# Layer 1's activation h·cos h with one pass fewer: turns, a saturating add, no Abs

## The chip, the cores and the metric
The kernel runs on one core of a Trainium2 chip. The time is device microseconds of that core; before it is the median of three runs. Engines are named as in the profile: PE is TensorE's matmul, PEld its weight load, DVE is VectorE, ACT is ScalarE, POOL is GpSimd, SP is SyncE, which issues the transfers.

## What is computed
```python
# q, k, v: 4 batches, 8 heads, 576 positions, 64 dims; w_in 512x2048, w_out 2048x512 per layer
scores = (1 / 8) * q @ k.T
ret = (scores * Dmat) @ v            # Dmat[i, j] = gamma_h ** (i - j) for i >= j, else 0
x = ret as 2304 x 512
h = x @ w1_in;  x = (h * np.cos(h)) @ w1_out                            # layer 1
h = x @ w2_in;  out = (np.maximum(h, 0) + np.log1p(np.exp(-abs(h)))) @ w2_out   # layer 2, a softplus
```

## The kernel before
Every product is made as three products of rounded parts (a high part and a low part, `h` and `l` in the names), so each value that enters a product is first split: ACT copies the high part, DVE or POOL subtracts to get the low one (`sub`, the row of line 317 in DVE's and POOL's lists).

The program has four stretches. First the attention, in 16 tiles of heads that go alone (0 to about 50 us) and 16 more woven in between what follows. Then the first four of sixteen column blocks of layer 1's hidden width, in five groups of tokens (`slot`: 12 matmuls into a PSUM bank called ha, hb, s or o, the activation, then 12 matmuls `acc<-gh,wh`), to about 200 us. Then the other twelve blocks of layer 1 as phase 0 of a scheme that makes 7 products in place of 8 (`quad`: seven groups of six matmuls, `ha<-x,pair`, `hb`, `s`, with additions on DVE and copies `cv` on ACT between them; `unit`: the output products `acc<-gh,pair`), to about 455 us. Then layer 2 in phases 1 and 2, to the end. `x_load` brings x for a phase and makes its sums (`tt`, 768 columns wide, POOL or DVE) and their splits (`x<-tt`).

The activation of layer 1 (`activate`) takes five passes for a bank. `a1` (line 792, ACT): ek = the nearest integer to h/2π. `a2` (796, DVE): er = h − 2π·ek. `a4` (800 on ACT or 803 on DVE): er = |er|. `a5` (806, ACT): sin(π/2 − er), which is cos h. `a6` (809, DVE): the product with h, into the bank (or g, gs). Then `parts` splits the product (835 on ACT, 317 on DVE) for the output matmuls. A DVE, ACT or POOL instruction runs when those before it on its engine are done, so the order of each engine's list decides who waits.

That order comes from a planner (`Plan`): each operation has an engine, a cost, a key (the time by which it is wanted) and its dependencies, and the planner lays out the whole program, the earliest possible start first and the lower key where two are equal. Operations marked POOL_DVE or ACT_DVE go to the engine that the planner's weights (`FLEX`, `FLEX_AD`) favour. The keys hang on the constants at the head of the file; a changed cost or constant can move instructions anywhere in the program.

Of the kernel before, what the change touches and what calls it, by code (L numbers as in the profile page):

```python
# [6 lines left out]

F32 = mybir.dt.float32
F32R = mybir.dt.float32r
I32 = mybir.dt.int32  # L10
U8 = mybir.dt.uint8
AF = mybir.ActivationFunctionType
ALU = mybir.AluOpType
# [14 lines left out]
NS = 9  # L28
HALF_PI = 1.5707963267948966
TWO_PI = 6.283185307179586  # L30
INV_TWO_PI = 0.15915494309189535


def t_mm(n):
# [8 lines left out]
def t_act(n, psum=False):  # L43
    return n / 1400.0 + (0.112 if psum else 0.154)


def t_dve(n):
    return n / 960.0 + 0.068


def t_dve2(n):
    return n / 1920.0 + 0.068
# [8 lines left out]
ACT_DVE = "act or dve"  # L61
# [4 lines left out]
    return layer == 2 or f < FA  # L66


FLEX = 0.801
FLEX_AD = 3.625  # L70
FLEX_2 = 50.0
ROOM = 258.786
SPARE = 1.248
# [6 lines left out]
GB = 2  # L80
PT = 3
R0 = 26.837
WB = (15.287, 22.043)
W3 = (33.576, 10.601, 12.195, 17.928, 32.155)
XW = 15.342
XC = 10.125
LAG_C = 1.399
LAG_S = 0.9
TT = 3
CA = (25.491, 78.45, 5.426, 6.897)  # L90
TURN = 0.6
XS = 51.626
FILL = (2, 5)
EARLY = 17.347
EARLY_2 = 7.642
AHEAD = {}
GAP = 2.0
LO_A = "pool or dve"
END = 3.1
LC = 8.411  # L100
LT = ("o", "s")
OFF = (4.42, 9.944, 21.033, 32.756)
LL = 12.0
LB = 1.9
WARM = 350
DX = 24.051
LEAD = 7.302
W0 = (46.735, 4.788, -1.046)
M0 = 28.072
AK = (4.689, 2.701)  # L110
PAIR_A = 1.48
# [4 lines left out]
SCALE = "pool"  # L116
KK = 1.331
KQ = -0.176
TIE = -8.152
LAG = -3.047  # L120
LEAD_G = 12.021
CX = 0.925
GT = (4, 7)
LS = 9
LEAD_S = 9.902
W4 = (-17.423, -10.623, 13.552, 0.176, 3.559)
W5 = (15.081, 16.579, 8.481, 12.575, 8.762)
PAD = 192
QS = 3

# [1 line left out]
class Plan:  # L132
# [10 lines left out]
    def op(self, eng, dur, key, fn, r=(), w=(), new=(), port=False, nbytes=0):  # L143
        i = len(self.ops)
        deps = set()
        for t in r:
            deps.update(self.writers.get(t, ()))
            self.readers.setdefault(t, []).append(i)
        for t in w:
            deps.update(self.writers.get(t, ()))  # L150
            deps.update(self.readers.get(t, ()))
            self.writers[t] = [i]
            self.readers[t] = []
        for t in (*r, *w):
            self.users.setdefault(t[0], []).append(i)
        for tag, bufs, tile_key in new:
            self.rings.setdefault(tag, (bufs, []))[1].append((i, tile_key))
        deps.discard(i)
        self.ops.append([eng, dur, key, fn, deps, port, nbytes])
        return i  # L160

    def order(self):
# [32 lines left out]
        for _ in range(n):  # L195
            best = None
            for i in can:
                eng, dur, key, _, _, uses_port, _ = self.ops[i]
                if eng == POOL_DVE:
                    f = max(ready[i], port)  # L200
                    t, d, e = min(
                        ((max(f, free[e]), d, e) for e, d in (("pool", t_pool(dur)), ("dve", t_dve(dur)))),
                        key=lambda o: o[0] + (FLEX if ready[i] < ROOM else FLEX_2 if ready[i] < ROOM_3 else FLEX_3) * o[1])
                elif eng == ACT_DVE:
                    t, d, e = min(
                        ((max(ready[i], free[e], port if e == "dve" and uses_port else 0.0), d, e) for e, d in zip(("act", "dve"), dur)),
                        key=lambda o: o[0] + FLEX_AD * o[1] + (SPARE if o[2] == "dve" else 0.0))
                else:
# [57 lines left out]
def retention_moe_moe(ctx, tc, qkv, w1, w2, mask, mtail, dq, dk, out):  # L266
    nc = tc.nc
# [16 lines left out]
    cst = apool("cst", 1)  # L284
# [4 lines left out]
    op = plan.op  # L289
# [11 lines left out]
    hp_t = small.tile([128, 1], F32, name="hp_t")  # L301
# [41 lines left out]
    CM = [M[-1] - TIE]  # L343
    MB = M[-1] + OFF[-1] + LL + 6.0
    for ph in range(3):
# [126 lines left out]
    def weight_out(q, key):  # L472
# [271 lines left out]
    def x_store(m):  # L744
        n, r0, xk = GROUPS[m], R[m], ("x", "a", m)
        for g in range(2):
            dma(lambda g=g: xd[g][:, :, r0:r0 + n], lambda g=g: T[xk][g][:, :, 0:n].bitcast(F32), 512 * n * 4, M[m] + XS + g, r=XT[m], w=[("xd", g, m)])

# [35 lines left out]
    def activate(layer, e, h_k, n, i, K1, dst=None, g_k=None, g_new=(), need=()):  # L784
        kk, rk = ((g, "m", i) for g in ("ek", "er"))
        k_k, r_k = (kk,), (rk,)
        tmp = lambda g, dt=F32: ew.tile([128, n], dt, tag=g, name=g, padded_shape=[128, 512])
        H_ = lambda: e["h"][:, 0:n]
        if layer == 1:
            def a1():  # L790
                e["k"] = tmp("ek", I32)
                nc.scalar.activation(e["k"], H_(), AF.Copy, scale=INV_TWO_PI)

            def a2():
                e["r"] = tmp("er")
                nc.vector.scalar_tensor_tensor(e["r"], e["k"], -TWO_PI, H_(), ALU.mult, ALU.add)  # L796

            def a4(eng):
                if eng is nc.scalar:
                    nc.scalar.activation(e["r"], e["r"], AF.Abs)  # L800
                else:
                    r = e["r"].bitcast(I32)
                    nc.vector.tensor_scalar(r, r, 0x7FFFFFFF, None, ALU.bitwise_and)

            def a5():
                nc.scalar.activation(e["r"], e["r"], AF.Sin, bias=hp_t[:, 0:1], scale=-1.0)  # L806

            def a6():
                nc.vector.tensor_tensor(dst() if dst else H_(), H_(), e["r"], ALU.mult)  # L809

            op("act", t_act(n, True), K1 + 0.1, a1, r=h_k, w=[k_k], new=[("ek", 2, kk)])
            op("dve", t_dve(n), K1 + 0.6, a2, r=h_k + [k_k], w=[r_k], new=[("er", 2, rk)])
            op(ACT_DVE, (t_act(n), t_dve2(n)), K1 + 1.4, a4, r=[r_k], w=[r_k], port=True)
            op("act", t_act(n) + 0.1, K1 + 1.5, a5, r=[r_k, ("cst", "hp")], w=[r_k, ("sin",)])
            op("dve", t_dve(n), K1 + 2.3, a6, r=[r_k, *(h_k if dst else []), *need], w=g_k or h_k, new=g_new)
            K2 = K1 + 2.8
        else:
            for to, z, g_k, g_new, mem in dst if isinstance(dst, list) else [(dst, slice(0, n), g_k, g_new, ())]:
                def a1(to=to, z=z):
                    d = to()  # L820
                    h_ = H_()[:, z]
                    nc.scalar.activation(d, h_ if d.ndim == 2 else h_.rearrange("p (u c) -> p u c", u=2), AF.Softplus)

                o_ = op("act", t_act(z.stop - z.start, True), K1 + 0.1, a1, r=[*h_k, ("ln",)], w=g_k, new=g_new)
                early.extend((o_, m) for m in mem)
            return
        if not dst:
            return parts(e, H_, h_k, n, i, K2, True)

# [106 lines left out]
    def quad(ph, y, s):  # L936
# [43 lines left out]
        product(1, 1, K, True, True)  # L980
        op(ACT_DVE, both, K + DT - EARLY, keep(1, 0, "v"), r=[rk[1], ("qopen",)], w=[(cv, 0)], new=[("cv", 1, cv)])
        product(2, 2, K + DT, True, True)
        product(3, 5, K + 2 * DT, True, True)
        op("dve", t_dve(HN), K + 3 * DT - EARLY_2, lambda: nc.vector.tensor_tensor(R(2), R(2), c["v"][:, 0], ALU.add), r=[(cv, 0)], w=[rk[2]])
        op(ACT_DVE, both, K + 3 * DT - EARLY, keep(3, 0, "5"), r=[rk[3], ("qopen",)], w=[(cv, 0)])
        product(1, 6, K + 3 * DT)
        op(ACT_DVE, both, K + 4 * DT - EARLY, keep(1, 1, "v"), r=[rk[1]], w=[(cv, 1)])
        product(3, 3, K + 4 * DT)
# [233 lines left out]
    def weight_in_s(ph, y, s):  # L1222
# [148 lines left out]
    def moe_a(t, todo):  # L1371
# [168 lines left out]
    for i in range(P0):  # L1540
        k = M[0] + CA[0] + 4 * i * CA[2]
        job(k, convert_ahead, 1, FQ[0] + i, k, CA[2])
    for q in range(NP2):
        k = CM[0] + CA[1] + 4 * q * CA[3]
        job(k, convert_ahead, 2, q, k, CA[3])
    for ph in range(3):
        W = (W3, W4, W5)[ph]
        for y in range(nb):
            k = KI(ph, y, 0) - XC
            job(k, x_load, ph, y, k)  # L1550
            for s in range(NQ[ph]):
                job(KI(ph, y, s), quad, ph, y, s)
                job(KI(ph, y, s) - max(0.1, W[0] if y == 0 and s < 2 else W[1] if y == 0 or ph else XW), weight_in_s, ph, y, s)
                if not ph:
# [5 lines left out]
        for q in range(NQ[ph]):  # L1560
            if ph:
                job(key_s(ph, 0, 0, q) - max(W[4 if q > 1 else 2], 0.1), weight_out_s, ph, q)
            else:
                k = unit_key(0, 0, q) - W3[2]
                job(max(k, (MR if q < 2 else MB) + 0.01), weight_out, FQ[0] + q, k)
# [83 lines left out]
```

## Time and profile before
| | us |
|---|---|
| median of 3 runs | 846.39 (845.26 to 848.43) |
| the profiled execution, its time | 848.93 |
| the profiled execution, its span | 846.8 |
| PE busy in the span | 825.4 (97%) |
| DVE, ACT, POOL busy | 666.9, 550.7, 84.1 |

The time counts about 2.1 us outside of the span of instructions. The profiled execution is 2.5 us slower than the median.

### The profile page before, as it was taken

Reading aid. Unit: us, or ns where it says so; the run is one execution under the profiler, and the core shown is the slowest. Engines: PE = TensorE matmul, PEld = TensorE weight load, DVE = VectorE, ACT = ScalarE, POOL = GpSimd, SP = SyncE. Lnnn points to the kernel's source line nnn. Section 1 sums busy time; section 2 is a strip of 40 time slices with the busy share of each in tenths; the row PEclk is TensorE's granted clock in tenths of the full one; section 3 lists DMA queues with packets and bytes.
Section 4 is the critical chain, followed back from the end, with each engine's and each line's share of the span. In section 5 each row is a group of like instructions: output and inputs, shape, how many; then the busy total and the mean of one; then the engine's idle time right before and its main releaser. Section 6 shows DMA issues by size and latency. Waiting matters only on the chain.

```text
span 846.8 us, 15943 instructions
## 1 busy us (share of the span) xinstructions
PE 825.4 (97%) x5792; PEld 783.1 (92%) x5792; DVE 666.9 (79%) x1486; ACT 550.7 (65%) x1213; POOL 84.1 (10%) x105
## 2 busy tenths in 40 slices
PE   7989999999999999999998999999999999999996
PEld 5767788888999999999998999999999999999996
DVE  3788767978898756876677879779888999876786
ACT  1276655678988867887787767555565766545442
POOL 3522110320231010010101010000000000000000
PEclk9999999999999999999999999999999999999999
DMA  9787999899887878685957866616469584464321
GB/s 313 276 330 253 361 384 331 309 371 352 307 323 224 299 275 267 224 234 203 313 216 242 293 207 206 248 63 232 180 197 352 207 310 153 153 227 168 119 86 53
DMA packets 74654, 208.79 MB, mean 247 GB/s; under 512 B 6864, under 2 KB 30800, under 8 KB 70736
## 3 DMA queue, kind: packets, MB, share of 16 engines
q1 hardware_dynamic: 71120, 203.06, 66.5%
q0 software_dynamic: 3456, 4.72, 3.7%
q8 instruction: 45, 0.74, 0.4%
q14 instruction: 33, 0.27, 0.1%
HBM read 129.64 MB, written 78.12 MB: 245 GB/s over the span
## 4 chain that ended last, share of the span: by engine, by line
PE 68%; issue 17%; DVE 6%; DMA 4%; ACT 3%; POOL 1%; SPq 0%; POOLq 0%; DVEq 0%; ACTq 0%
PE acc L1092 20%; PE ha L963 15%; PE s L963 8%; PE acc L1318 7%; PE acc L856 4%; PE hb L963 4%; PE o L670 2%; PE ha L757 1%; DMA raw<-in_qkv 1%; PE hb L757 1%; POOL pd L1337 1%; PE s L593 1%; DMA pd<-pt 1%; DVE gl L317 1%; DVE pair L317 1%
## 5 line engine op out<-in xcount | busy, mean ns | idle before, releaser
L963 PE MATMUL ha<-x,pair 128*128 128x384 f32 x1008 | 203.7, 336 | 3.9 <-DVE g L809 2.1
L963 PEld LDWEIGHTS ha<-x,pair 128*128 128x128 f32 x1008 | 174.4, 188 | 7.2 <-DVE g L809 2.7
L1318 PE MATMUL acc<-gh,pair 128*128 128x384 f32 x576 | 157.1, 335 | 0.6 <-ACT pt L321 0.6
L1092 PE MATMUL acc<-pair,gh 128*128 128x256 f32 x576 | 113.2, 283 | 0.0
L1318 PEld LDWEIGHTS acc<-gh,pair 128*128 128x128 f32 x576 | 105.0, 188 | 1.0 <-ACT pt L321 0.9
L963 PE MATMUL s<-x,pair 128*128 128x384 f32 x504 | 101.3, 335 | 0.1
L1318 PE MATMUL acc<-gl,pair 128*128 128x384 f32 x288 | 96.3, 334 | 0.0
L1092 PEld LDWEIGHTS acc<-pair,gh 128*128 128x128 f32 x576 | 89.5, 191 | 0.4 <-ACT gh L1073 0.2
L963 PEld LDWEIGHTS s<-x,pair 128*128 128x128 f32 x504 | 88.2, 188 | 1.2 <-ACT cv L321 0.4
L1092 PE MATMUL acc<-pair,ah 128*128 128x256 f32 x432 | 86.7, 282 | 0.4 <-DVE pt L1171 0.4
L1092 PE MATMUL acc<-pair,gl 128*128 128x256 f32 x288 | 81.6, 283 | 0.5 <-DVE gl L317 0.5
L1092 PEld LDWEIGHTS acc<-pair,ah 128*128 128x128 f32 x432 | 70.0, 190 | 0.7 <-DVE pt L1171 0.6
L1092 PE MATMUL acc<-pair,al 128*128 128x256 f32 x216 | 61.1, 283 | 0.3 <-DVE al L317 0.3
L321 ACT ACTIVATE cv<-ha 128x384 f32<-128x384 f32 x84 | 41.1, 489 | 30.7 <-PE ha L963 30.1
L806 ACT ACTIVATE er<-er,hp_t 128x384 f32<-128x384 f32 (+1 forms) x92 | 57.6, 627 | 0.5
L1092 PEld LDWEIGHTS acc<-pair,gl 128*128 128x128 f32 x288 | 55.0, 191 | 1.1 <-DVE gl L317 1.1
L317 DVE TENSOR_TENSOR gl<-sf,gh 128x512 fp32r<-128x512 f32 x72 | 49.4, 689 | 8.1 <-ACT gh L1073 6.5
L1073 ACT ACTIVATE gh<-sf 128x512 fp32r<-128x512 f32 x72 | 45.3, 631 | 14.6 <-PE acc L1092 5.9
L1318 PEld LDWEIGHTS acc<-gl,pair 128*128 128x128 f32 x288 | 54.1, 188 | 0.1
L800 ACT ACTIVATE er<-er 128x384 f32<-128x384 f32 (+1 forms) x85 | 45.5, 540 | 11.7 <-DVE er L796 10.2
L963 PE MATMUL hb<-x,pair 128*128 128x384 f32 x252 | 50.7, 335 | 0.0
L1062 ACT ACTIVATE ah<-gs 128x384 fp32r<-128x384 f32 x60 | 31.5, 525 | 28.5 <-PE acc L1092 28.3
(210 smaller groups left out, 1718.3 us busy)
## 6 DMA issues: line engine op xcount, KB each, us to landing
wr<-in_w SPq DMA_DIRECT2D x64, 512.0 KB, 5.9
pair<-wpd SPq DMA_DIRECT2D x16, 1792.0 KB, 7.0
wpd<-pair SPq DMA_DIRECT2D x14, 1792.0 KB, 7.6
wd<-wk SPq DMA_DIRECT2D x56, 256.0 KB, 4.4
pair<-wd SPq DMA_DIRECT2D x36, 256.0 KB, 5.7
sd<-x SPq DMA_DIRECT2D x12, 768.0 KB, 3.5
x<-sd SPq DMA_DIRECT2D x12, 768.0 KB, 5.9
raw<-in_qkv SPq DMA_DIRECT2D x12, 640.0 KB, 6.5
```

What stands on the lines that cost most here:

```text
L317: e.tensor_tensor(out_, a, hi.bitcast(F32), ALU.subtract)
L321: nc.scalar.activation(out_, in_, AF.Copy)
L670: nc.tensor.matmul(o_at(z)[Z[j]], lhs(j), rhs(j), start=start, stop=stop, skip_group_check=True)
L757: nc.tensor.matmul(h_[:, 0:n], lhs, rhs[:, d, 0:n], start=(k == 0), stop=(k == 3 * NC - 1))
L800: nc.scalar.activation(e["r"], e["r"], AF.Abs)
L806: nc.scalar.activation(e["r"], e["r"], AF.Sin, bias=hp_t[:, 0:1], scale=-1.0)
L856: nc.tensor.matmul(acc[o][:, 0:n], l[:, s], e[r], start=(first and z == 0), stop=(last and z == 2))
L963: nc.tensor.matmul(R(r), w_(a), x_(b), start=(start and n == 0), stop=(n == 5), skip_group_check=True)
L1062: nc.scalar.activation(A_(0), T[uk][:, 0:HN], AF.Copy)
L1073: nc.scalar.activation(T[hk], T[fk], AF.Copy)
L1092: nc.tensor.matmul(acc[m][:, i * 256:i * 256 + 256], l[p], r[o], start=(s == 0 and i == 0 and n == 0), stop=(s == half_p - 1 and n == 2), ...
L1318: nc.tensor.matmul(acc[m][:, 0:HN], l[:, z_], e[r], start=(first and z == 0), stop=(last and z == 2))
```

## The change
h is made in turns: the tables by which the scores are multiplied carry a further factor 1/(2π), so layer 1's h arrives as h/2π. `a1` then copies −h − 0.25 to the nearest integer ek. `a2` is one custom DVE instruction, TENSOR_ADD_SAT: er = ek + h, held between −0.75 and 0.25. `a5` takes sin(2π·er + π/2), whose argument lies within ±π. `a4` is gone. Layer 1's output is smaller by 2π, and layer 2's softplus multiplies it back by its `scale`. And some thirty numbers among the planner's constants are others (two pairs are shown).

```diff
+from concourse.dve_ops import TENSOR_ADD_SAT
...
+TURN_MIN, TURN_MAX = -0.74999994, 0.24999997
...
-FLEX = 0.801
-FLEX_AD = 3.625
+FLEX = 1.332
+FLEX_AD = 3.856
...
-LEAD_G = 12.021
-CX = 0.925
+LEAD_G = 7.778
+CX = 0.855
...
-                nc.scalar.activation(e["k"], H_(), AF.Copy, scale=INV_TWO_PI)
+                nc.scalar.activation(e["k"], H_(), AF.Copy, bias=-0.25, scale=-1.0)
...
-                nc.vector.scalar_tensor_tensor(e["r"], e["k"], -TWO_PI, H_(), ALU.mult, ALU.add)
-
-            def a4(eng):
-                if eng is nc.scalar:
-                    nc.scalar.activation(e["r"], e["r"], AF.Abs)
-                else:
-                    r = e["r"].bitcast(I32)
-                    nc.vector.tensor_scalar(r, r, 0x7FFFFFFF, None, ALU.bitwise_and)
+                nc.vector._custom_dve(TENSOR_ADD_SAT, out=e["r"], in0=e["k"], in1=H_(), s0=TURN_MAX, s1=TURN_MIN)
...
-                nc.scalar.activation(e["r"], e["r"], AF.Sin, bias=hp_t[:, 0:1], scale=-1.0)
+                nc.scalar.activation(e["r"], e["r"], AF.Sin, bias=hp_t[:, 0:1], scale=TWO_PI)
...
-            op(ACT_DVE, (t_act(n), t_dve2(n)), K1 + 1.4, a4, r=[r_k], w=[r_k], port=True)
...
-                    nc.scalar.activation(d, h_ if d.ndim == 2 else h_.rearrange("p (u c) -> p u c", u=2), AF.Softplus)
+                    nc.scalar.activation(d, h_ if d.ndim == 2 else h_.rearrange("p (u c) -> p u c", u=2), AF.Softplus, scale=TWO_PI)
...
-    mask = np.where(rel >= 0, gam[:, None, None] ** np.maximum(rel, 0), 0.0) * 0.125
+    mask = np.where(rel >= 0, gam[:, None, None] ** np.maximum(rel, 0), 0.0) * (0.125 / TWO_PI)
...
-    dq = by_row[:, :, None] ** (np.arange(320) % 128)[None, None, :] * 0.125
+    dq = by_row[:, :, None] ** (np.arange(320) % 128)[None, None, :] * (0.125 / TWO_PI)
```

In the lists of instructions of the two programs, 92 of `a4` (85 on ACT, 7 on DVE) are gone and 92 of `a2` stand as ISA rows. Of operations that may run on POOL or DVE, the five 768-wide sums that `x_load` had on POOL are on DVE now, and so are four of the attention's key scalings (`raw<-raw,dk_t`); one low part of a weight (`wl<-wk,wh`) went to POOL. PE's list differs in some hundred places, all of them moved groups of the same matmuls; its last 222 rows are the same.

The first place is on DVE, near 158 us, where layer 1's slots s and o pass through the activation while x for phase 0 arrives. Before:
```order
L796 SCALAR_TENSOR_TENSOR er<-ek,s 128x384
L317 TENSOR_TENSOR pair<-tt,pair 128x768
L317 TENSOR_TENSOR pair<-pair 128x512
L317 TENSOR_TENSOR pair<-tt,pair 128x256
L809 TENSOR_TENSOR s<-s,er 128x384
L796 SCALAR_TENSOR_TENSOR er<-ek,o 128x384
L1471 TENSOR_TENSOR tt<-x 128x768
L410 SCALAR_TENSOR_TENSOR wk<-wr_1851,wk 128x512
L317 TENSOR_TENSOR gl<-s,gh 128x384
L809 TENSOR_TENSOR o<-o,er 128x384
```
After the change:
```order
L797 ISA er<-ek,s 128x384
L318 TENSOR_TENSOR pair<-pair 128x512
L318 TENSOR_TENSOR pair<-tt,pair 128x768
L803 TENSOR_TENSOR s<-s,er 128x384
L1464 TENSOR_TENSOR tt<-x 128x768 x2
L797 ISA er<-ek,o 128x384
L1464 TENSOR_TENSOR tt<-tt 128x768
L318 TENSOR_TENSOR gl<-s,gh 128x384
L803 TENSOR_TENSOR o<-o,er 128x384
```
Two `tt<-x` now stand ahead of `er<-ek,o`, and one `tt<-tt` behind it; the weight conversion `wk<-wr` and one 256-wide split have left the stretch ahead of `gl<-s`, and the two wide splits of `pair` have changed places.

The second place is on PE, near 205 us, in an early quad of phase 0, while layer 1's last token group of the first stretch is still woven in. Before (x18 are three products of six, one behind the other):
```order
L757 MATMUL s<-x,wl 128x512
L757 MATMUL s<-x,wh 128x512 x2
L757 MATMUL s<-x,wl 128x512
L963 MATMUL hb<-x,pair 128x384 x6
L963 MATMUL ha<-x,pair 128x384 x18
L963 MATMUL s<-x,pair 128x384 x6
```
After the change:
```order
L758 MATMUL s<-x,wh 128x512 x2
L758 MATMUL s<-x,wl 128x512
L849 MATMUL acc_2330<-gh,wh 128x512
L849 MATMUL acc_2330<-gl,wh 128x512
L849 MATMUL acc_2330<-gh,wl 128x512
L956 MATMUL ha<-x,pair 128x384 x6
L956 MATMUL hb<-x,pair 128x384 x6
L956 MATMUL ha<-x,pair 128x384 x6
L956 MATMUL s<-x,pair 128x384 x6
L956 MATMUL ha<-x,pair 128x384 x6
L956 MATMUL s<-x,pair 128x384 x6
```
The three products on bank ha are taken apart: a product on hb or s stands between each two.

The third place is on DVE, near 47 us, at the end of the attention that goes alone. Before:
```order
L403 SCALAR_TENSOR_TENSOR wk<-wy,wr_566 128x512
L317 TENSOR_TENSOR wl<-wk,wh 128x512
L620 TENSOR_TENSOR p<-s,m_t 128x256
L620 TENSOR_TENSOR p<-o,m_t 128x256
L652 SCALAR_TENSOR_TENSOR st<-st,dk_t,s 128x64
L317 TENSOR_TENSOR x<-acc_198,x 128x192
```
After the change:
```order
L404 SCALAR_TENSOR_TENSOR wk<-wy,wr_594 128x512
L564 TENSOR_TENSOR raw<-raw,dk_t 128x256
L621 TENSOR_TENSOR p<-s,m_t 128x256
L621 TENSOR_TENSOR p<-o,m_t 128x256
L653 SCALAR_TENSOR_TENSOR st<-st,dk_t,s 128x64
L318 TENSOR_TENSOR wl<-wk,wh 128x512
```
The split `wl` has moved behind the masks `p` and the state `st`, and a key scaling stands in its place.

## Rows read from the trace of the kernel before
**Rows 1.** head and section 1 of the page, busy time of each engine
```profile
span 846.8 us, 15943 instructions
...
PE 825.4 (97%) x5792; PEld 783.1 (92%) x5792; DVE 666.9 (79%) x1486; ACT 550.7 (65%) x1213; POOL 84.1 (10%) x105
```
**Rows 2.** windows: PE, PEld, DVE, ACT, POOL busy, clock, DMA share, GB/s
```profile
40.00:60.00 20.00, 17.64 (x213) 13.48 (x210) 16.41 (x49) 13.18 (x35) 4.80 (x6) 0.91 0.81 300
...
160.00:170.00 10.00, 7.98 (x36) 7.41 (x35) 9.00 (x15) 4.38 (x9) 2.14 (x1) 0.83 1.05 419
170.00:280.00 110.00, 106.94 (x569) 99.25 (x568) 94.94 (x166) 96.37 (x200) 22.50 (x21) 1.00 0.91 312
280.00:440.00 160.00, 160.00 (x924) 159.61 (x923) 112.12 (x202) 127.03 (x258) 10.73 (x12) 1.00 0.75 252
440.00:480.00 40.00, 37.66 (x214) 36.70 (x214) 29.81 (x61) 29.11 (x64) 3.55 (x4) 1.00 0.79 248
480.00:820.00 340.00, 340.00 (x2384) 339.80 (x2383) 286.42 (x692) 201.77 (x478) 3.52 (x4) 1.00 0.56 200
820.00:846.80 26.80, 19.96 (x151) 18.34 (x149) 20.23 (x55) 7.24 (x14) 0.00 (x0) 0.97 0.20 70
```
**Rows 3.** waits of PE: total us, times, longest
```profile
PE s L593 <- DVE st L652: 2.3, 1, 2.3
PE ha L963 <- DVE g L809: 2.1, 2, 1.1
PE acc L856 <- ACT gh L835: 1.9, 1, 1.9
...
PE acc L856 <- DVE gl L317: 1.2, 3, 0.8
PE ha L963 <- ACT cv L321: 1.2, 2, 0.6
```
**Rows 4.** lines by form: the activation's passes, busy and mean ns
```profile
L800 ACT ACTIVATE er<-er 128x384 f32<-128x384 f32 x73 | 38.0, 525 | 8.2 <-DVE er L796 6.8
...
L796 DVE SCALAR_TENSOR_TENSOR er<-ek,hb 128x384 f32<-128x384 int32 x21 | 11.6, 552 | 7.5 <-ACT ek L792 7.4
...
L803 DVE TENSOR_SCALAR er<-er 128x384 int32<-128x384 int32 x7 | 2.5, 359 | 0.2
```
**Rows 5.** windows of L800 (the Abs pass) alone, ACT busy
```profile
160.00:280.00 120.00, 17.05 (x32) 0.99 0.92 321
```
**Rows 6.** timeline around the wait at 164: start us, us, engine, operation
```profile
158.31 2.15 DVE L317 TENSOR_TENSOR pair<-tt,pair 128x768 fp32r<-128x768 f32 x1
...
160.99 0.41 DVE L317 TENSOR_TENSOR pair<-tt,pair 128x256 fp32r<-128x256 f32 x1
...
162.26 0.95 DVE L1471 TENSOR_TENSOR tt<-x 128x768 f32<-128x768 f32 x1
...
163.12 0.68 DVE L410 SCALAR_TENSOR_TENSOR wk<-wr,wk 128x512 int32<-128x512 int32 x1
...
164.19 0.56 DVE L317 TENSOR_TENSOR gl<-s,gh 128x384 fp32r<-128x384 f32 x1 [0.38 <-ACT gh L835]
...
164.20 0.44 PE L856 MATMUL acc<-gh,wh 128*128 128x384 f32 x1 [1.87 <-ACT gh L835]
```
**Rows 7.** timeline around the wait at 49
```profile
46.36 0.42 DVE L563 TENSOR_TENSOR raw<-raw,dk_t 128x256 f32<-128x256 f32 x1
...
47.80 0.94 DVE L317 TENSOR_TENSOR wl<-wk,wh 128x512 fp32r<-128x512 f32 x1
...
49.70 0.37 PE L593 MATMUL s<-raw 64*128 64x128 f32 x1 [2.31 <-DVE st L652]
```
**Rows 8.** timeline around the wait at 252
```profile
247.87 1.85 POOL L1471 TENSOR_TENSOR tt<-tt 128x768 f32<-128x768 f32 x1 [1.77 <-DVE tt L1471]
...
248.21 1.93 DVE L317 TENSOR_TENSOR gl<-g,gh 128x384 fp32r<-128x384 f32 x1
...
252.94 1.31 PE L963 MATMUL ha<-x,pair 128*128 128x384 f32 x6 [0.95 <-DVE g L809]
```

More of the change, by code (lines that the diff above doesn't have):

```diff
@@ L30 @@
 TWO_PI = 6.283185307179586
-INV_TWO_PI = 0.15915494309189535
+TURN_MIN, TURN_MAX = -0.74999994, 0.24999997
 def t_mm(n):
@@ L82 @@
 R0 = 26.837
[L83 to L86, printed above, removed]
+WB = (16.86, 21.855)
+W3 = (33.511, 10.601, 12.203, 18.951, 18.328)
+XW = 18.07
+XC = 10.621
 LAG_C = 1.399
@@ L89 @@
 TT = 3
-CA = (25.491, 78.45, 5.426, 6.897)
+CA = (23.719, 78.45, 5.342, 4.584)
 TURN = 0.6
-XS = 51.626
+XS = 51.414
 FILL = (2, 5)
-EARLY = 17.347
-EARLY_2 = 7.642
+EARLY = 13.944
+EARLY_2 = 7.188
 AHEAD = {}
@@ L101 @@
 LT = ("o", "s")
-OFF = (4.42, 9.944, 21.033, 32.756)
+OFF = (-1.482, 9.944, 20.766, 32.756)
 LL = 12.0
@@ L107 @@
 LEAD = 7.302
-W0 = (46.735, 4.788, -1.046)
+W0 = (46.735, 4.788, -0.157)
 M0 = 28.072
@@ L118 @@
 KQ = -0.176
-TIE = -8.152
-LAG = -3.047
-LEAD_G = 12.021
-CX = 0.925
+TIE = -8.153
+LAG = -3.013
+LEAD_G = 7.778
+CX = 0.855
 GT = (4, 7)
 LS = 9
-LEAD_S = 9.902
-W4 = (-17.423, -10.623, 13.552, 0.176, 3.559)
-W5 = (15.081, 16.579, 8.481, 12.575, 8.762)
+LEAD_S = 10.241
+W4 = (-20.151, -10.623, 13.343, -5.177, 13.791)
+W5 = (15.439, 17.479, 8.363, 12.575, 2.839)
 PAD = 192
@@ L812, in activate @@
             op("dve", t_dve(n), K1 + 0.6, a2, r=h_k + [k_k], w=[r_k], new=[("er", 2, rk)])
-            op(ACT_DVE, (t_act(n), t_dve2(n)), K1 + 1.4, a4, r=[r_k], w=[r_k], port=True)
-            op("act", t_act(n) + 0.1, K1 + 1.5, a5, r=[r_k, ("cst", "hp")], w=[r_k, ("sin",)])
-            op("dve", t_dve(n), K1 + 2.3, a6, r=[r_k, *(h_k if dst else []), *need], w=g_k or h_k, new=g_new)
-            K2 = K1 + 2.8
+            op("act", t_act(n) + 0.1, K1 + 1.2, a5, r=[r_k, ("cst", "hp")], w=[r_k, ("sin",)])
+            op("dve", t_dve(n), K1 + 1.9, a6, r=[r_k, *(h_k if dst else []), *need], w=g_k or h_k, new=g_new)
+            K2 = K1 + 2.4
         else:
```

## The prediction
> **What bounds the kernel now.** First the busy times of the page [rows 1]: PE works 825.4 of 846.8 us, DVE 666.9, ACT 550.7. The matmuls are the same before and after, so the change can only give back PE time that is lost to waiting, and 21.4 us is all that PE's busy time leaves. Then where that lies, by windows [rows 2]. From 280 to 440 and from 480 to 820 us PE is busy in 160.00 of 160 and 340.00 of 340 us: nothing can be won there, though ACT spends much of the first on the pass that goes. PE idles 2.36 us from 40 to 60, 2.02 from 160 to 170, 3.06 from 170 to 280, 2.34 from 440 to 480, and 6.84 in the last 26.8 us, which are layer 2's end. The rest is the start. In the stretch from 160 to 280, where layer 1's first blocks, phase 0 and the arrival of x overlap, DVE is busy 103.94 and ACT 100.75 of 120 us: two engines nearly full, with PE waiting for one or the other. The waits by name [rows 3] say so: 2.3 us once for the state `st` (DVE), 1.9 once for `gh` (ACT), 1.2 in three for `gl` (DVE), 2.1 in two for `g` (DVE), 1.2 in two for the copies `cv` (ACT).
>
> Two of the windows also show a lower granted clock [rows 2]: 0.91 over 20 us and 0.83 over 10 us. At 1.2 instead of 2.4 GHz that is 1.8 and 1.7 us of matmul time lost. The first stands behind PE's wait of 2.31 us [rows 7], the second behind the one of 1.87 us [rows 6]; from 170 to 280, whose longest wait is the 0.95 us of [rows 8], the clock reads 1.00.
>
> **What goes, and what comes for it.** The Abs pass is 525 ns on ACT at 384 columns, and where DVE did it 359 ns [rows 4]; 92 passes go, and with them a hand-over in each chain. From 160 to 280 us that is 17.05 us in 32 passes [rows 5], so ACT's 100.75 falls to about 84 of 120. `a1`, `a5` and the softplus keep their instructions with other constants: I take nothing. The tables carry other numbers of the same size: nothing.
>
> TENSOR_ADD_SAT stands in the place of the multiply-add and reads the same two operands. No row shows it. The nearest is the instruction that it replaces, 552 ns [rows 4]; the upper end is that and another pass over the tile, 552 + 359 = 911 ns, if the clamp is not free. I take 552, since operands, width and count are the same, and keep 911 for a rival.
>
> Five 768-wide sums go from POOL to DVE: 5 x 0.95 [rows 6] = 4.75 us more on DVE. Against it stand two DVE instructions that lay beside such a sum on POOL and took far longer than their like: `gl<-g` 1.93 us [rows 8] where `gl<-s` takes 0.56 [rows 6], and `pair` 2.15 where another 768-wide pass takes 0.95 [rows 6]. That gives 1.37 + 1.20 = 2.57 us back, so DVE's queue grows by some 2.2 us net. The Trainium skill's page SBUF — State Buffer (section Who interferes with whom) says that a DVE instruction with two SBUF inputs and a POOL instruction that reads SBUF block one another fully until the first has finished; the two slow rows agree. By that rule each of the five sums can block DVE for its whole 1.85 us [rows 8], 9.3 us in all, and the move would free 4.5 us of DVE instead of costing 2.2; the forecast would be some 2 us lower.
>
> **The waits one by one, in the new order.**
> - The 1.87 us at 164.20 [rows 6]. PE waits for the split of slot s, and goes on only with its `gl`. In the old list DVE runs `pair` (2.15), a narrow split (0.41), `tt<-x`, `wk` (0.68), then idles 0.38 for `gh`, whose engine still had Abs ahead of it. In the new list the block, the narrow split, `wk` and the idle time are gone ahead of `gl<-s`, 1.20 + 0.41 + 0.68 + 0.38 = 2.67 us, and two more sums stand there, 2 x 0.95 = 1.90. PE goes on 0.8 us earlier. This is the place where what ACT gives, DVE takes back.
> - The longest wait for `gl`, 0.8 us [rows 3], near 180: the slot of 512 columns on bank o is multiplied four output groups earlier in the new list, so its chain has time. I count 0.8.
> - The two waits for `cv`, 1.2 us [rows 3], near 208: three products on bank ha stood one behind the other, each waiting until ACT had copied the last, with Abs and others on ACT. Now a product on hb or s stands between. I count 1.2.
> - The wait for `g` at 252.94, 0.95 us [rows 8]: its chain went through the blocked `gl<-g` (1.37 lost) and an Abs (0.53). Both go, a sum of 0.95 comes: 1.37 + 0.53 - 0.95 = 0.95. I count all of it.
> - The other wait for `g`, 1.1 us [rows 3], near 453, the end of layer 1: one Abs pass less in its chain, 0.5 us; DVE's queue there keeps the rest.
> - The 2.31 us at 49.70 [rows 7]: `wl` (0.94) leaves the place ahead of the masks, a scaling (0.42) comes: 0.5 us.
>
> Together 0.8 + 0.8 + 1.2 + 0.95 + 0.5 + 0.5 = 4.75 us.
>
> **The clock.** The two long waits shrink to about 1.8 and 1.1 us, between the 1.87 after which the clock fell and the 0.95 after which it did not. Ends: nothing, or 3.5 us. I take one of the two, 1.7 us.
>
> **New waits.** The order changes at some hundred places of PE's list, and any of them may be late. Ends: nothing, or one as long as the longest now, 2.3 us. I take the middle, 1.2. From 480 to 820 us I take nothing, since PE never waits there and only groups are exchanged; the last 222 rows of PE's list are the same, so the end keeps its 6.84 us. If a key has put a transfer of layer 2 late, that cover is gone and PE shows it there at full price.
>
> **Sum:** 4.75 + 1.7 - 1.2 = 5.25 us. Against the profiled execution's own 848.93 that is 843.7; the profiled one lies 2.5 us over the median of the runs shown, 846.39, so the median comes to **841.1 us** (0.6% less). A measurement of this kernel can hardly tell less than 0.5%, 4.2 us, from no change.
>
> **Rivals.**
> - *DVE was the limit, and ACT's relief is lost.* For it: DVE is as full as ACT, the two longest waits of [rows 3] name DVE, and DVE's queue grows by 2.2 us. Then of the waits only the two for `cv` go, no clock comes back, and the new waits cost their 1.2: about 846, no change. Against it: the chain of each activation is shorter by a pass and a hand-over, whoever is full.
> - *Far more comes back.* The new order was laid for the shorter chains. All waits from 40 to 60, 160 to 280 and 440 to 480 gone is 2.36 + 5.08 + 2.34 = 9.8 us, both losses of clock 3.5: 833 at the end, 835 with a little left. [...]
> - *The custom instruction is dear, and the kernel slower.* If TENSOR_ADD_SAT costs 911 ns instead of 552, the 32 of the stretch from 160 to 280 bring 11.5 us to DVE, on top of 103.94 + 2.2: 117.6 of 120, a full queue under every chain. PE then waits for most of the added time, some 10 us, the gains above but for `cv` are gone, and the kernel comes to about 854. It turns slower than before from about 0.75 us on, where half of the free 16 us of DVE is used up. Against it: same operands, same width.
>
> **Chances.** The forecast's case (4.75 us of waits with the clock and the new waits between their ends: 4.75 + 3.5 = 8.25 less, to 4.75 - 2.3 = 2.45 less, so 838.1 to 843.9) 0.48, of which about a quarter ends within 0.5%; no change 0.27; far more 0.13; slower 0.12. Faster by over 0.5%: 0.36 + 0.13 = 0.49; within: 0.12 + 0.26 = 0.38; slower: 0.12 and a stray 0.01. The range that leaves 2 in 10 out, half of the dearest cases on both sides: 836 to 849.
>
> **What would show it.** Right: ACT without its Abs rows and some 45 us less busy; ISA rows near 550 ns; no wait for `cv` near 205; the wait near 164 at about 1.1 us; granted clock above 0.9 from 160 to 170; PE still 340.00 of 340 from 480 to 820. Wrong: ISA rows of 0.8 us or more; a wait behind the two `tt<-x` near 162 as long as before; DVE above 115 us from 160 to 280; a new wait of 2 us with a fall of the clock anywhere; PE waiting in layer 2.

## The result

The changed kernel takes 839.28 us (median of five, 838.98 to 841.43), beside it the kernel before 848.43 (five, 845.26 to 849.38); the ratio is 0.991, 95% interval 0.988 to 0.994. Timed a second time, on another occasion, it took 839.11 (four, 837.80 to 839.76) with a ratio of 0.990 (0.988 to 0.992). So it is faster by some 1%. The forecast had 841.1, 0.6% less than before, with most of the gain in PE's waits.

The head and the busy times of the changed kernel's page answer to [rows 1]:
```profile
span 837.5 us, 15905 instructions
...
PE 822.0 (98%) x5792; PEld 781.4 (93%) x5792; DVE 666.0 (80%) x1487; ACT 515.1 (62%) x1128; POOL 72.3 (9%) x97
```
ACT works 35.6 us less, DVE as long as before. The windows of the changed kernel, with the columns of [rows 2], say where PE loses less time:
```profile
40.00:60.00 20.00, 17.90 (x207) 13.60 (x206) 16.59 (x47) 14.59 (x37) 5.16 (x7) 0.91 0.88 336
...
160.00:170.00 10.00, 9.25 (x46) 7.96 (x46) 10.00 (x14) 5.66 (x10) 0.00 (x0) 1.00 1.05 428
170.00:280.00 110.00, 108.45 (x588) 102.42 (x587) 96.56 (x174) 86.80 (x175) 16.01 (x17) 1.00 0.92 326
...
440.00:480.00 40.00, 39.79 (x229) 39.30 (x228) 31.64 (x70) 28.88 (x68) 3.54 (x4) 1.00 0.88 297
480.00:820.00 340.00, 339.55 (x2399) 338.69 (x2398) 287.44 (x699) 198.28 (x469) 3.54 (x4) 1.00 0.54 192
```
PE's idle time falls from 2.02 to 0.75 us (160 to 170), from 3.06 to 1.55 (170 to 280) and from 2.34 to 0.21 (440 to 480): 4.9 us. From 40 to 60 it falls by 0.3. The fall of the clock behind 164 is gone, 1.7 us. Of the 0.45 us that PE idles from 480 to 820, where it idled nothing before, 0.20 is a new wait, for a copy `cv` at 513.54; the other 0.25 is a wait for `gl` that the kernel before has at 824.03, and that now comes at 814.69, inside the window. The last 26.8 us idle 7.12 in place of 6.84. In sum that is 4.9 + 0.3 + 1.7 - 0.2 - 0.3 = 6.4 us. Some more lies in the matmuls right behind a wait, which last 0.44 us in place of 0.33 (timeline below), so that fewer waits also mean fewer slow ones.

The start is a matter of the single execution. By the same view, the first 40 us of the kernel before:
```profile
0.00:40.00 40.00, 35.48 (x480) 26.38 (x482) 20.87 (x72) 8.15 (x25) 19.48 (x36) 0.96 0.86 310
```
The same program, executed once more:
```profile
0.00:40.00 40.00, 36.48 (x506) 27.25 (x508) 21.87 (x76) 8.20 (x26) 19.55 (x36) 1.00 0.85 310
```
The changed kernel:
```profile
0.00:40.00 40.00, 36.41 (x510) 27.32 (x512) 22.40 (x76) 8.29 (x27) 19.52 (x37) 1.00 0.85 310
```
And the changed kernel once more, with the stretch behind it:
```profile
0.00:40.00 40.00, 35.80 (x474) 26.92 (x476) 20.65 (x70) 8.13 (x25) 19.25 (x36) 0.96 0.87 310
40.00:60.00 20.00, 17.89 (x233) 13.69 (x231) 16.95 (x51) 13.80 (x36) 5.79 (x8) 1.00 0.85 323
```
Each program has a fall of the clock there in one execution and none in the other. In the two with a fall PE waits 1.69 and 1.70 us for `raw` at 19 us, in the two without 0.81 and 0.79. Of the 9.65 us between the two profiled executions (848.93 and 839.28) about 2.5 are of this kind: 0.93 of idle time and 0.04 x 40 = 1.6 of clock. With the 6.4 above that is 8.9. The ratios, over many executions, are the measure: 0.9 to 1.0% of 847 is 7.7 to 8.5 us.

### The profile page after: what moved, and what is told of

It reads as the page before. It is cut to its first block, busy times and chain, and to the rows that moved or that the text cites. A ratio compares the mean times of both kernels' runs of the same rounds, so it can differ in the third digit from the quotient of the medians.

```text
span 837.5 us, 15905 instructions
## 1 busy us (share of the span) xinstructions
PE 822.0 (98%) x5792; PEld 781.4 (93%) x5792; DVE 666.0 (80%) x1487; ACT 515.1 (62%) x1128; POOL 72.3 (9%) x97
## 4 chain that ended last, share of the span: by engine, by line
PE 84%; DVE 9%; DMA 2%; issue 2%; ACT 1%; SPq 0%; POOL 0%; POOLq 0%; DVEq 0%; ACTq 0%
PE acc L1085 19%; PE ha L956 19%; PE acc L1311 16%; PE s L956 10%; PE acc L849 5%; PE hb L956 4%; PE ha L758 2%; PE hb L758 2%; PE o L671 2%; DVE gl L318 1%; PE s L594 1%; DVE pair L318 1%; DVE x L318 1%; DVE tt L1464 1%; DMA dq_t<-in_dq 1%
## 5 line engine op out<-in xcount | busy, mean ns | idle before, releaser
L800 ACT ACTIVATE er<-er,hp_t 128x384 f32<-128x384 f32 (+1 forms) x92 | 57.9, 630 | 15.9 <-DVE er L797 14.6
L392 ACT ACTIVATE wy<-wr 128x512 f32<-128x512 f32 x64 | 43.0, 672 | 17.4 <-DVE wk L407 6.7
L318 DVE TENSOR_TENSOR al<-gs,ah 128x384 fp32r<-128x384 f32 x60 | 33.3, 556 | 21.6 <-ACT ah L1055 21.6
```

Of the source, the lines that this page charges most:

```text
L318: e.tensor_tensor(out_, a, hi.bitcast(F32), ALU.subtract)
L392: nc.scalar.activation(y, T["wr", u][:, :, 1].bitcast(F32), AF.Prelu, scale=2.0 ** -112, alpha=2.0 ** 32)
```

## The experiments

None of the kernels leaves work of the reference out. PE's idle us in the three stretches where the changed kernel gains, worked out from the windows (length less PE's busy time), stand beside the times. "Old order" is the order of instructions of the kernel before, "new order" that of the changed kernel. The stretches are fixed in time, so in a slower kernel the same work stands later in them:

| kernel | median us | ratio to before (95%) | 160–170 | 170–280 | 440–480 |
|---|---|---|---|---|---|
| before | 847 to 848 | 1 | 2.02 | 3.06 | 2.34 |
| before, again | 848.0 (one) | | 1.89 | 3.11 | 2.34 |
| changed | 839.3 | 0.991 (0.988–0.994) | 0.75 | 1.55 | 0.21 |
| changed, again | 839.1 | 0.990 (0.988–0.992) | 0.78 | 1.56 | 0.20 |
| old order, no pass | 846.2 | 0.999 (0.998–1.001) | 1.54 | 3.44 | 1.80 |
| new order, a pass put back | 861.9 | 1.018 (1.016–1.020) | 1.01 | 7.62 | 1.34 |
| new order, dearer add | 862.8 | 1.019 (1.016–1.021) | 1.78 | 7.42 | 1.78 |
| new order, sums on POOL | 842.8 | 0.995 (0.993–0.997) | 0.76 | 3.24 | 0.20 |
| no pass, planned by old keys | 844.8 | 0.997 (0.996–0.998) | 1.80 | 2.44 | 1.22 |
| pass kept, planned by new keys | 853.0 | 1.007 (1.005–1.009) | 1.79 | 7.16 | 1.76 |
| old order, no pass, sums on DVE | 847.2 | 1.000 (0.999–1.001) | 1.38 | 3.56 | 2.45 |
| changed, masks first | 841.4 | 0.994 (0.991–0.996) | 0.71 | 1.54 | 0.21 |
| changed, two places put right | 837.9 | 0.989 (0.987–0.990) | 0.72 | 1.08 | 0.20 |

The waits repeat: two executions of one program agree within 0.13 us in every one of the three stretches.

**The pass alone, in the old order.**
```diff
-                nc.vector.scalar_tensor_tensor(e["r"], e["k"], -TWO_PI, H_(), ALU.mult, ALU.add)
+                nc.vector._custom_dve(TENSOR_ADD_SAT, out=e["r"], in0=e["k"], in1=H_(), s0=TURN_MAX, s1=TURN_MIN)
...
             def a4(eng):
-                if eng is nc.scalar:
...
+                pass
```
The constants are those of the kernel before, and the planner still books the pass, which now does nothing, so every list keeps its order.

> The kernel before with its own order kept instruction for instruction, and of the change only this: the Abs pass is left out, the saturating add and the new constants stand in place of the old. It tells the shorter chain from the new order. If the forecast's account holds (the pass is worth what it leaves in each chain, and the rest comes from what the new order puts elsewhere), the wait at 164 loses only the 0.38 us that DVE stood idle for `gh`, the two waits for `g` near 253 and 453 lose 0.53 us each, the two for `cv` about half of their 1.2: 2.0 us in all, ratio 0.9975 to the kernel before, about 846 where that is at 848; the clock still falls behind the wait at 164. If the shorter chain alone earned the gain, it comes to 839 to 841 (0.991) with both orders alike. If the new order alone did, it stays within 0.5 us of the kernel before. From 440 to 480 us PE's idle time, 2.34 before and 0.21 after, goes with the order or with the pass, and this run shows which. From 0 to 47 us the order is that of both kernels: a start with a fall of the clock at 19 us is the kernel before's own, one without it a matter of the single execution.

It gains nothing that can be told: 0.999, with an interval that ends at 0.998. Near 164 the freed ACT gives `gh` earlier, and DVE's list has the same instructions as before ahead of `gl`. Its timeline there (start, duration, engine, operation, idle time and releaser):
```profile
161.14 0.41 DVE L318 TENSOR_TENSOR pair<-tt,pair 128x256 fp32r<-128x256 f32 x1
...
162.41 0.95 DVE L1468 TENSOR_TENSOR tt<-x 128x768 f32<-128x768 f32 x1
...
163.27 0.68 DVE L411 SCALAR_TENSOR_TENSOR wk<-wr,wk 128x512 int32<-128x512 int32 x1
...
163.56 0.45 PE L853 MATMUL acc<-gh,wh 128*128 128x384 f32 x1 [1.07 <-ACT gh L832]
163.88 0.55 DVE L318 TENSOR_TENSOR gl<-s,gh 128x384 fp32r<-128x384 f32 x1
...
164.47 0.44 PE L853 MATMUL acc<-gl,wh 128*128 128x384 f32 x1 [0.47 <-DVE gl L318]
```
The wait of 1.87 us is now 1.07 for `gh` and 0.47 for `gl`: 0.33 gained, as expected of the 0.38. The waits for `gl` near 180 (0.81) and for `cv` (0.58 twice) stand as before. `g` at 252 costs 0.21 where it was 0.95 [rows 8], and a new wait of 1.13 for `o` stands 7 us ahead of it. The same timeline shows where that one comes from, and the wait for `g` at 453, for which 0.53 less was expected:
```profile
242.18 2.55 POOL L1468 TENSOR_TENSOR tt<-x 128x768 f32<-128x768 f32 x1
242.96 2.18 DVE L318 TENSOR_TENSOR gl<-g,gh 128x384 fp32r<-128x384 f32 x1
...
245.67 1.34 PE L960 MATMUL ha<-x,pair 128*128 128x384 f32 x6 [1.13 <-DVE o L990]
...
452.96 0.61 PE L960 MATMUL ha<-x,pair 128*128 128x384 f32 x2 [1.15 <-DVE g L806]
```
A `gl` now stands beside a POOL sum and takes 2.18 us where the one at 243.30 in the kernel before took 1.10, and `o` comes late behind it. The wait at 453 has not moved. A shorter chain moves some waits; in this order nothing is gained by it.

**The pass back, and a dearer add, in the new order.**
```diff
+                nc.scalar.activation(e["r"], e["r"], AF.Copy)
                 nc.scalar.activation(e["r"], e["r"], AF.Sin, bias=hp_t[:, 0:1], scale=TWO_PI)
```


> The changed kernel with its order kept, and one more pass on ACT in the place where Abs stood: the tile er copied onto itself ahead of the sine, in all 92 chains. ACT grows by 92 x 0.525 = 48 us, by 16 to 17 in the stretch from 160 to 280 us, where it is busy 92.5 of 120: some 109 of 120, more than the kernel before had. If the pass matters for its place in the chain (the forecast), the waits come back that the forecast counts with an Abs in their chain: those near 164, 253 and 453 by 0.5 us each, `cv`, and ACT's full queue adds more: 3 to 8 us, 842 to 847. If the new order earned the gain by itself, it stays within 1 us of the changed kernel, 838 to 841.


```diff
                 nc.vector._custom_dve(TENSOR_ADD_SAT, out=e["r"], in0=e["k"], in1=H_(), s0=TURN_MAX, s1=TURN_MIN)
+                nc.vector.tensor_scalar(e["r"], e["r"], TURN_MAX, TURN_MIN, ALU.min, ALU.max)
```


> The changed kernel with its order kept, and a second pass on DVE behind each saturating add: the same clamp once more on the tile er, in place, which does not alter the values. It makes the saturating add as dear as the upper end of the forecast's bound, some 0.9 us in place of 0.55. DVE grows by about 11.5 us from 160 to 280, from 106.6 to 118 of 120. The rival of the dear instruction puts such a kernel at 854, where the kernel before has 848: some 10 us or more above the changed kernel's 839. If DVE had room, the chains grow by 0.36 us each and the sum of that at the four places where PE waits for a chain is 1.5 us: 840 to 842.

Both cost far more than their expectations had: some 23 us above the changed kernel for 521 ns on ACT in 92 chains, and some 24 for 379 ns on DVE (means at 384 columns), a quarter of a microsecond for each pass. The windows with the pass back:
```profile
170.00:280.00 110.00, 102.38 (x531) 92.01 (x529) 91.80 (x160) 93.17 (x189) 14.81 (x16) 1.00 0.83 297
280.00:440.00 160.00, 155.62 (x871) 150.39 (x872) 103.85 (x187) 126.18 (x254) 11.45 (x13) 1.00 0.78 261
```
and with the dearer add:
```profile
170.00:280.00 110.00, 102.58 (x530) 92.67 (x529) 100.70 (x186) 78.84 (x157) 15.39 (x16) 0.99 0.83 297
280.00:440.00 160.00, 157.08 (x887) 152.83 (x886) 118.27 (x232) 111.31 (x219) 11.49 (x13) 1.00 0.81 264
```
Neither engine is full: ACT has 93 of 110 in the one, DVE 101 of 110 in the other. PE waits even from 280 to 440, where the kernel before, with the pass in, had no wait at all [rows 2]. The waits by name say for what. With the pass back:
```profile
PE ha L957 <- DVE g L804: 4.8, 7, 1.2
```
and in the changed kernel:
```profile
PE ha L956 <- DVE g L803: 0.2, 1, 0.2
```
PE waits at the ends of chains, as it would if this order were laid close to chains of four passes and each longer one made the next instruction in some list late. That it is the chain's length, and not the work added to an engine's list, is not shown: both kernels add both. PE's idle time is also not the whole cost. Over the whole span it grows from 15.5 us to 30.0 and 28.9; PE's busy time grows by 8.5 and 10.7, for the same 5792 matmuls.

**The square of activation and keys.** In the changed kernel, all nineteen constants of the change put back (two are shown):
```diff
-FLEX = 1.332
+FLEX = 0.801
...
-LEAD_G = 7.778
+LEAD_G = 12.021
```


> The changed kernel with all keys and costs of the kernel before: the planner knows that the pass is gone and lays its order anew, but nothing is chosen for it. The kernel before is at 847, the one with the old order and no pass at 846, the changed kernel at 839. If the gain comes from an order that is laid by a planner that knows the shorter chains, this kernel has most of it: 839 to 843. If it comes from the choice of the keys, a new order by the old keys is a draw like any other: 844 to 850, with waits of 1 us and more in places where neither kernel has one.

In the kernel before, the same constants set to the new values, and nothing else:
```diff
-FLEX = 0.801
+FLEX = 1.332
...
-LEAD_G = 12.021
+LEAD_G = 7.778
```


> The kernel before, Abs pass and all, with the keys and costs of the changed kernel; the planner lays the order with the pass in it. With the run above it makes the square of old and new activation by old and new keys. If the new keys are good by themselves (what they put elsewhere, the sums on DVE among it), it lies below the kernel before: 841 to 845. If keys fit only the chains for which they were chosen, it is no better than the kernel before, more likely worse: 847 to 855.

With no pass, planned by the old keys: 0.997. The new keys with the pass: 1.007. Both together: 0.990. The planner alone finds a third of the gain; the keys by themselves do harm, 6 us; the rest is that these keys and these chains go together. Each of the four is one order, and how much of its time is that order's luck is not shown.

**The five sums.** In the new order back to POOL, then in the old order to DVE:
```diff
             def run(e):
...
+                if ph == 0 and y < 2 and (i == 0 or (i == 3 and y == 0 and o_ == ALU.subtract)):
+                    e = nc.gpsimd
```


> The changed kernel with its order kept, and the five 768-wide sums of phase 0 back on POOL where the kernel before had them. By the forecast's account DVE loses 4.75 us of work and gets back some 2.6 us of being held up beside POOL; at the wait near 164 two sums of 0.95 leave the queue ahead of gl, and a held-up instruction of 1.2 us and a later `tt` come: PE's wait there changes by less than 0.7 us, the whole by less than 1 us: 838.5 to 840.5. If a sum on POOL holds DVE up for its whole 1.85 us (9.3 us for five), DVE's queue is worse by 4.5 us net, and it comes to 841 to 844, with DVE instructions near 2 us beside the POOL rows. If DVE is what limits the stretch, it gets faster, by up to 2 us: 837 to 838.


```diff
+                e = nc.vector if ph == 0 else e
```


> The kernel with the old order and without the pass (846.2), and one thing more: the five 768-wide sums of phase 0 that POOL did there are on DVE. It shows the move apart from all others. In the changed kernel the way back cost 3.5 us, though the forecast had less than 1. If POOL beside DVE is what costs (two rows of 1.93 and 2.15 us in the kernel before, where their like take 0.56 and 0.95), those rows fall to 0.6 and 0.95 here and it gains 1 to 3 us: 843 to 845. If the added 4.75 us of DVE's own weigh as much, it stays at 845.5 to 847. By the forecast's account the wait near 164, 1.54 us in the kernel with the old order, changes by 1.20 less and 0.95 more.

On POOL they cost 3.5 us: more than the forecast's account, and within what the expectation had for DVE being held up for a POOL row's whole length. The timeline with the sums on POOL:
```profile
160.88 1.83 POOL L1466 TENSOR_TENSOR tt<-tt 128x768 f32<-128x768 f32 x1 [0.96 <-DVE tt L1466]
161.29 0.56 DVE L318 TENSOR_TENSOR gl<-s,gh 128x384 fp32r<-128x384 f32 x1
...
238.57 1.82 POOL L1466 TENSOR_TENSOR tt<-x 128x768 f32<-128x768 f32 x1
238.63 2.18 DVE L318 TENSOR_TENSOR gl<-g,gh 128x384 fp32r<-128x384 f32 x1
...
240.86 0.45 PE L1311 MATMUL acc<-gl,pair 128*128 128x384 f32 x1 [1.18 <-DVE gl L318]
```
One `gl` beside a POOL sum takes 0.56 us, the other 2.18: the first reads a PSUM bank (s) and one tile in SBUF, the second two tiles in SBUF. And PE waits 1.18 us for the second, a wait that the changed kernel lacks. Smaller waits come as well, among them 0.49 for a copy `pt` at 159.94 and 0.52 for `cv` at 173.44; that they too come from POOL holding DVE up is not shown. In the old order the move takes such slow rows away (`gl` at 243 from 2.18 to 0.55, at 249 from 2.03 to 0.55), and the wait of 1.13 for `o` with them. It changes nothing in the time, 1.000, for a wait of the same size comes elsewhere in its timeline:
```profile
176.10 1.32 PE L960 MATMUL s<-x,pair 128*128 128x384 f32 x6 [1.24 <-ACT cv L322]
```
The same move is worth 3.5 us in the one order and nothing in the other.

**Waits in layer 0, and two places put right.**
```diff
+        run = self.order()
+        move = [267, 269, 268, 270]
+        run = [i for i in run if i not in move]
+        at = run.index(223)
+        run[at:at] = move
```
The four numbers are the two masks, the state's copy and its sum; 223 is the `wk` pass.

> The changed kernel with four instructions put earlier: the two masks, the state's copy and its sum that PE waits for at 47.80 us (2.0 us, the longest wait of layer 0) come ahead of a `wk` pass of 0.69 us and a scaling of 0.68 us on DVE. The wait should be 0.5 us or less. Behind it the clock falls from 48.6 to 52.0 us in the changed kernel, which is 1.7 us of matmul time. If the fall hangs on the length of this wait, it goes with it and the kernel gains 3 us: 836 to 837. If the clock falls at that place whatever the wait, the gain is 1.5 us: 837.5 to 838.5. If what is put behind comes too late in turn, it shows as a new wait within 3 us, and nothing is gained.

The wait goes from 2.05 to 0.77 us, and nothing is gained. The timeline with the masks first:
```profile
45.95 1.28 POOL L323 TENSOR_TENSOR wl<-wk,wh 128x512 fp32r<-128x512 f32 x1
46.03 1.75 DVE L409 SCALAR_TENSOR_TENSOR wk<-wy,wr 128x512 int32<-128x512 int32 x1
46.17 0.37 PE L599 MATMUL s<-raw 64*128 64x128 f32 x1 [0.77 <-DVE st L658]
...
50.37 0.70 PE L763 MATMUL ha<-x,wh 128*128 128x512 f32 x2 [2.30 <-DVE x L323]
```
The `wk` that was put behind now meets a POOL row and takes 1.75 us in place of 0.69; the splits of x stand behind it, and PE waits 2.30 us for them. The next kernel puts twelve operations of those splits ahead too, and one split near 247 (1280, `pair<-wr,pair`) from POOL to DVE:
```diff
-        move = [267, 269, 268, 270]
+        move = [267, 269, 268, 270, 271, 273, 275, 277, 279, 281, 272, 274, 276, 278, 280, 282]
...
+        self.eng[1280] = "dve"
```


> The changed kernel with two places put right by hand. At 47 us the masks, the state and the six splits of x that PE waits for go ahead of a `wk` pass and a scaling (the kernel with the masks alone put ahead lost 2.3 us again at the splits, behind that `wk`, which ran into a POOL pass and took 1.75 us). At 247 us the 512-wide split of a pair goes from POOL to DVE, where it costs 0.68 us and `gl` beside it 0.56 in place of 1.65. If the places are worth what their rows show, PE starts layer 1's first product 2 us earlier, the wait of 0.84 us at 250 falls to 0.4, and the kernel gains 2.4 us, with the fall of the clock near 50 us up to 4: 835 to 837. If the next instruction in the queue is late in turn, as with the masks alone, it gains less than 1 us: 838.5 to 841.

At both places the waits get shorter. Its timeline at 47 us:
```profile
46.34 0.37 PE L600 MATMUL s<-raw 64*128 64x128 f32 x1 [0.78 <-DVE st L659]
...
48.17 0.73 PE L764 MATMUL ha<-x,wh 128*128 128x512 f32 x2
```
and near 249:
```profile
246.44 0.55 DVE L324 TENSOR_TENSOR gl<-g,gh 128x384 fp32r<-128x384 f32 x1
...
249.20 0.61 PE L962 MATMUL ha<-x,pair 128*128 128x384 f32 x2 [0.34 <-DVE o L992]
```
The first product of layer 1 starts without a wait, PE waits 0.78 us for the state, as with the masks alone, and the wait at 250 falls from 0.84 to 0.34. In all it is 837.85 us beside 839.11 for the changed kernel in the same set of runs: 1.3 us, half of the 2.4 expected, with intervals that overlap (0.987 to 0.990 and 0.988 to 0.992). It is the lowest median here, but not by more than these runs can tell.

**The same programs again.**

> The changed kernel once more, unaltered, timed beside the kernel before. In the profiled executions so far PE's loss from 0 to 40 us differs by some 4 us between kernels that have the same instructions there, and the clock falls near 20 us in some and not in others. If that is a matter of the single execution, this run repeats every wait of the changed kernel from 160 us on to 0.1 us, while the start differs by up to 2 us; the ratio to the kernel before stays at 0.989 to 0.993. If the changed kernel's start is its own gain, the start too repeats, with no fall of the clock near 20 us.

> The kernel before once more, unaltered, for a second profile. It tells which of its marks are its own: the falls of the clock near 20, 50 and 166 us, the waits of 1.9 us at 164 and of 1.1 and 0.65 us near 453. If the fall near 166 belongs to the order of the work there, it is here again, with 0.83 from 160 to 170; if it is a matter of chance, as the kernels with 1.4 and 1.8 us of idle time there and no fall suggest, it may be missing. The waits stay.

The waits repeat, the start does not, and the clock near 50 us does not either. The changed kernel's second execution has this row in its timeline:
```profile
49.75 0.37 PE L594 MATMUL s<-raw 64*128 64x128 f32 x1 [2.04 <-DVE st L653]
```
The wait is as long as in the first, 2.04 us beside 2.05, and the granted clock of 40 to 60 us is 1.00 (above) where the first had 0.91. From 160 to 170 us both executions of the kernel before read 0.83 and both of the changed kernel 1.00.

## Why the prediction was right, and where its sizes were off

**Right: the place.** PE's work is unchanged, and the gain lies in three of the four stretches that the forecast named. In the fourth, near 49 us, the wait for `st` went from 2.31 to 2.05 where the forecast counted 0.5. ACT's busy time falls (by 35.6 us, not 45: the records of ACT's neighbouring instructions overlap, so 45.6 us of passes are less of busy time), and from 160 to 280 us it is 92.5 where the forecast had about 84. The saturating add costs what the multiply-add cost [rows 4], by the lines of the changed kernel, grouped by form:
```profile
L797 DVE CUSTOM_DVE_ANT_0 er<-ek,hb 128x384 f32<-128x384 int32 x21 | 11.6, 553 | 5.9 <-ACT ek L793 5.8
L797 DVE CUSTOM_DVE_ANT_0 er<-ek,ha 128x384 f32<-128x384 int32 x21 | 11.6, 550 | 4.3 <-ACT ek L793 4.0
```

**Right, and too small: the wait at 164**, forecast 0.8 us shorter, at about 1.1. PE waits 0.49 there now, for `gl` alone, 1.4 shorter. The changed kernel's timeline has the sums ahead of `gl` and no DVE instruction held up by POOL, as the 2.67 less 1.90 supposed, but two of the three sums run before `gh` is wanted at all and stand in nobody's way:
```profile
157.40 1.90 DVE L1464 TENSOR_TENSOR tt<-x 128x768 f32<-128x768 f32 x2
...
159.68 0.94 DVE L1464 TENSOR_TENSOR tt<-tt 128x768 f32<-128x768 f32 x1
...
160.22 0.44 PE L849 MATMUL acc<-gh,wh 128*128 128x384 f32 x1
160.55 0.54 DVE L318 TENSOR_TENSOR gl<-s,gh 128x384 fp32r<-128x384 f32 x1
...
161.15 0.45 PE L849 MATMUL acc<-gl,wh 128*128 128x384 f32 x1 [0.49 <-DVE gl L318]
...
161.43 0.34 PE L849 MATMUL acc<-gh,wl 128*128 128x384 f32 x1
```

**Right in sum, from 170 to 280.** The forecast had 0.8 + 1.2 + 0.95 = 2.95 for three waits there, less 1.2 for new ones: 1.75. The idle time falls by 1.5. The waits for `gl` near 180, for `cv` near 208 and for `g` at 252 go. The first two went by the order, as the forecast had it: in the old order without the pass they stay. New ones come, the longest 0.84 for `o` at 250 and 0.38 for `gl` at 202.80. In layer 2, where the forecast took nothing, 0.20 us came.

**Mis-sized: the end of layer 1**, the term of 0.5 us for "one Abs pass less in its chain". At that place two waits, 1.79 us, go and one of 0.21 comes: 1.6 us. A wait of 0.55 for `pt` at 465.80 goes too, which makes the 2.1 of the window. The kernel before, at this place:
```profile
452.50 0.55 DVE L809 TENSOR_TENSOR g<-ha,er 128x384 f32<-128x384 f32 x1
...
453.10 0.62 PE L963 MATMUL ha<-x,pair 128*128 128x384 f32 x2 [1.14 <-DVE g L809]
...
454.37 0.98 PE L963 MATMUL ha<-x,pair 128*128 128x384 f32 x4 [0.65 <-DVE pair L317]
```
and the changed one:
```profile
443.37 0.56 DVE L803 TENSOR_TENSOR g<-ha,er 128x384 f32<-128x384 f32 x1
...
445.32 0.44 PE L1311 MATMUL acc<-gl,pair 128*128 128x384 f32 x1 [0.21 <-DVE gl L318]
...
448.89 1.20 PE L956 MATMUL ha<-x,pair 128*128 128x384 f32 x6
```
The six matmuls that need bank ha free and the new `pair` start 5.0 us after `g` is done now, and PE works at output products in between. The forecast looked at the chain alone and passed over PE's own row that moved. That it is the order, and not the pass, the old order without the pass shows: the waits of 1.15 and 0.65 us stand there as before, and what its window gains, 2.34 to 1.80, is the wait for `pt`. With the pass put back into the new order PE waits 1.19 for `gh` at the end of layer 1 (1.34 idle in the window), so the order needs the shorter chain.

**Wrong as a reason: what a shorter chain gives.** The step that took 0.5 us off the two waits for `g`, for the Abs in their chains, was put as if the pass gave it. In the old order without the pass the wait at 453 is 1.15 us, as before, and what the one at 252 loses, 0.74, comes back as 1.13 for `o`. By itself the pass gives nothing that can be told (0.999); new order and shorter chain together give 1%.

**Not shown: the clock.** The forecast took one of two falls back, 1.7 us, for waits that get shorter than some length between 0.95 and 1.87 us. The fall at 166 did go in both executions of the changed kernel. But the length of the wait does not decide it. The kernel with the pass kept and planned by new keys has this wait, and the window around it reads 1.00:
```profile
163.99 0.73 PE L757 MATMUL o<-x,wh 128*128 128x512 f32 x2 [1.79 <-DVE gl L317]
...
160.00:170.00 10.00, 8.21 (x43) 7.39 (x43) 10.00 (x14) 6.26 (x12) 0.00 (x0) 1.00 1.04 408
```
The old order without the pass has waits of 1.07 and 0.47 there and reads 0.83; and near 50 the same wait of 2.0 us has a fall in one execution and none in the other. What does decide it stays open, and that the term of 1.7 us came out is luck. The other part of the sum, waits less new waits, was forecast at 3.55 us and is about 4.7 between the two profiles (the 6.4 above less the clock's 1.7).

**The rivals.** DVE as the limit: no, though its 106.6 of 120 us are more than before. Far more: the waits of 160 to 280 fell by half, not to nothing. A dear instruction: it is not dear; but its price was put too low. The forecast had about 854 for 0.36 us more (its own terms, 846.4 and 10 less the 1.2 for `cv`, make 855), and a turn to slower from 0.75 us on, 0.2 more than the 0.55 it takes; measured it is 862.8 for some 0.38 us more, and by that slope the 8 us gained would be used up at some 0.13 us more, an estimate from that one point. DVE's free time was the wrong measure for it.

**The block of DVE by POOL.** The forecast kept its 2.2 us and gave the rule of the Trainium skill's page SBUF — State Buffer (section Who interferes with whom) as another account, 2 us lower. With the sums on POOL in the new order the kernel is 3.5 us slower, so the rule's account was the nearer there; in the old order the move changes nothing, and neither account shows in the time. The rule also says which DVE instructions it strikes, those with two inputs in SBUF; the `gl` of 0.56 us with one input in PSUM and the `gl` of 2.18 us with two tiles in SBUF agree.

## What to carry to other kernels

In a program whose order is laid out for its chains, a pass taken out of a chain can give nothing until the order is laid anew for it (0.999 here), and one put in can cost far more than the engine's free time suggests (0.25 us for each pass of 0.4 to 0.5 here, with the engines at 85 to 92%). To price such a change, look at the rows that move on the engine that waits, PE's own first, and not only at the chain. When a stall is taken away, read what comes next in the same list: with the masks put first, the splits of x behind them were late by more than was gained (2.30 us for 1.28).

## What was not expected of the hardware

- The same program, executed twice, differs by 1.0 us of PE's busy time in the first 40 us and by whether the granted clock falls near 20 and near 50 us; its waits from 160 us on repeat within 0.13 us.
- TENSOR_ADD_SAT, a custom DVE instruction on two operands, takes 550 to 553 ns at 384 columns, and the multiply-add on the same operands 552.
- A `wk` pass on integers, 0.69 us alone, took 1.75 us beside a POOL pass of 1.28.
